# One comparison per candidate, batch-wise gate columns, and another order of the last batch's steps, between attention and its experts

## The chip, the core and the metric

The kernel runs on one core of a Trainium2 chip. The core has five engines with instruction queues of their own: TensorE (PE: matrix multiplications; its loads of weights are shown apart, as PEld), VectorE (DVE), ScalarE (ACT), GpSimd (POOL) and SyncE (SP, which here only issues transfers). Each engine works through its queue in order. SBUF is the working memory of 128 partitions, PSUM holds what TensorE writes, and HBM holds inputs, outputs and the scratch `xs`. The metric is the device time of one execution in microseconds.

## The reference

Block-causal attention over 8 batches of 8 heads, 576 positions and 64 columns, and behind it a mixture of 8 experts, in which each token goes to one expert and each expert keeps at most 80 tokens, those with the largest gates. `x` is attention's output, as 4608 tokens of 512 columns.

```
scores = scale * np.matmul(q, k.transpose(0, 1, 3, 2))
mask = block_i >= block_j                      # blocks of 64 positions
scores = np.where(mask, scores, -1000000000.0)
attn = np.exp(scores - max);  attn = attn / (sum(attn) + 1e-09)
x = np.matmul(attn, v)                         # (4608, 512) after a transpose
...
logits = x @ w_gate
expert_idx = np.argmax(logits, axis=1)
gate_w = softmax(logits)[np.arange(N), expert_idx]
for e in range(E):
    tok_idx = np.where(expert_idx == e)[0]
    if len(tok_idx) > capacity:
        keep = np.argpartition(-gw, capacity)[:capacity]
        tok_idx = tok_idx[keep]
    h = np.maximum(x[tok_idx] @ w1[e], 0.0)
    out[tok_idx] = gate_w[tok_idx, None] * (h @ w2[e])
```

All other rows of the output are zero.

## The kernel before

**Attention.** Two heads form a pair; 32 pairs go through a software pipeline. A table of steps (`TURN`, `LAST` for the last pair) sets the order in which the code issues each step of the pairs in flight: transposes of q and k on VectorE, scores on TensorE, row maxima on VectorE, exponentials on ScalarE, transposes of the probabilities on TensorE, their copies out of PSUM on ScalarE or VectorE (`take`, line 784), products with v. At "t" in the table (function `t`, line 843) a batch's small steps of the gate run one at a time, from the list `small`. A pair's result is transposed on VectorE (`flip`, line 407) and four transfers per batch, on SyncE's queue, store it in `xs` (`store_x`, line 420). The softmax's division is not done there: `xs` also gets the reciprocals of the sums.

**Gates.** For each batch the logits per token are made (`products`, `shift`, `expo`), the chosen expert is marked (`first_of`: `eq` is 1 for the first largest) and the gate weighted (`weight`). `turn` or, for the last batch, `turn_gated` spreads gates over lanes into the tile `sp`, and `turn2` brings them by matmuls to PSUM, so that 16 partitions hold one expert's gates. `placed` (line 578) copies them into `Wt`. `Wt` has the gates of all batches in two halves h of 160 columns, in the order t, batch, a.

**Router, from line 971.** After the last batch, per partition and half: MAX8 takes the 8 largest gates of 160 (line 981), 6 of them are candidates, 12 in all (`NCAND`). Their places come from max_index (line 1011). `spread` and six matmuls (line 1004) put all 192 candidates of an expert next to each other in PSUM. For each candidate one pass counts the larger ones, six on VectorE (line 1049) and six on ScalarE (line 1053, a sum of signs, which is twice the count and an offset). The count, with a penalty for empty candidates and an order among equals (`pen`), is the slot. `one_hot` compares three candidates' slots at a time with 0 to 79 (line 1060, fp32, result bf16). Twelve matmuls with these (line 1079) pick per slot and expert the token's number, split in RI's parts hi and lo, which GpSimd makes from the place by shifts, products and sums. Line 1083 adds them: `gi`.

**Gathers and the start of the experts.** GpSimd gathers an expert's 80 rows of `xs` by `gi` (`fetch`, line 1093), for experts 0, 1 and 2 at once. VectorE splits the gates in three bf16 parts, TensorE picks them with the same one-hots (line 1120), ScalarE copies the result (gsum) and VectorE sums it to `comb` (lines 1133 and 1134). `divide` (line 1197) multiplies an expert's gathered rows by the reciprocals: four instructions each. For expert 0 these are ordered behind the sum in `comb` (line 1263), and four transposes, four copies on ScalarE and 64 matmuls follow, piece by piece. For expert 1 (`split`, line 1256) nothing in the code holds them behind expert 0's; the framework's scheduler places them, and all other instructions of this part, in VectorE's queue. `finish_` (line 1145) makes flags (`ids`, `vm`, `chk`, `dif`) that tell whether the 12 candidates were enough; if not, a general path runs. It doesn't run here.

**Experts.** For each: 128 matmuls with w1, ScalarE's relu, the matmuls with w2, a gated sum and a scatter on GpSimd's queue. Weights come in 2 MB transfers on SyncE's queue, three of the sixteen during attention, the first of the others behind the gather of expert 0.

**Warm-ups.** `warm` (line 788) issues matmuls of no use, 512 columns each, between steps of the router. `WARM` lists how many: at the kernel's start, behind the turn of batch 6, of batch 7, behind the ranking, behind the pick of tokens and behind the pick of gates; `WARM_PICK` stands in the middle of the pick.

## Time and profile before

| | |
|---|---|
| median of 3 runs | 382.70 us (382.64 to 382.75) |
| the profiled execution | 382.09 us, span 380.4 us |
| attention | to about 273.5 us |
| router, to expert 0's first matmul | 273.5 to 290.9 us |
| experts | 290.9 to 374 us |
| last scatter, to the end | from 375.05 us |
| busy share of the span | TensorE 96%, VectorE 75%, ScalarE 75%, GpSimd 48% |

The span is the time from the first to the last recorded instruction; the execution has 1.7 us around it. Times in the views are microseconds from the span's start. A line of the timeline gives the start, the busy time, engine, line, operation, output and inputs, how many instructions are merged, and in brackets how long the engine sat idle before it and what released it. Merged instructions overlap, so that two can be busy for less than the sum of both. In the windows PEclk is the clock that TensorE was granted, as a share of 2.4 GHz.

### The profile page before, as it was taken

What the parts mean: (1) busy time and instruction counts of PE and PEld (TensorE: products, weight loads), DVE (VectorE), ACT (ScalarE), POOL (GpSimd) and SP (SyncE); (2) the same over time, 40 slices, a digit from 0 to 9 for tenths busy, and PEclk for the clock granted to TensorE, in tenths of its full rate; (3) what the DMA queues carried; (4) which work ended last, traced back from release to release, by engine and by line L of the source; (5) the groups of instructions that cost most, each with busy time, mean ns of one, the idle gap of its engine ahead of it and who ended that gap; (6) DMA issues with size and microseconds to landing.
All of it is one profiled execution on the core that took longest, in us unless ns stands there. A gap on an engine that the chain in (4) does not pass through costs nothing.

```text
span 380.4 us, 15167 instructions
## 1 busy us (share of the span) xinstructions
PE 366.7 (96%) x5973; PEld 247.5 (65%) x5973; DVE 285.9 (75%) x804; ACT 286.9 (75%) x880; POOL 181.0 (48%) x373
## 2 busy tenths in 40 slices
PE   5899999999999999999999999999999999999993
PEld 3666667676676776676676676667667555666661
DVE  5889999999999999999999999999985311111001
ACT  1799999999999999999999999999521332322331
POOL 6346665656976766786577664431133112220000
PEclk9999999999999999999999999999999999999998
DMA  9979999999999999999999999999965999999940
GB/s 125 155 122 157 141 163 152 204 188 124 190 228 146 200 197 198 165 146 247 167 171 215 184 155 137 244 396 416 264 127 175 385 391 393 401 397 393 407 188 26
DMA packets 166272, 84.42 MB, mean 222 GB/s; under 512 B 132509, under 2 KB 151805, under 8 KB 166192
## 3 DMA queue, kind: packets, MB, share of 16 engines
q1 hardware_dynamic: 154768, 61.80, 75.4%
q0 software_dynamic: 9056, 21.27, 23.9%
q8 instruction: 49, 0.80, 1.0%
q10 hardware_dynamic: 2368, 0.30, 0.6%
q14 instruction: 31, 0.25, 0.3%
HBM read 63.21 MB, written 20.33 MB: 220 GB/s over the span
## 4 chain that ended last, share of the span: by engine, by line
PE 85%; DVE 8%; ACT 3%; DMA 2%; issue 1%; POOL 0%; POOLq 0%; ACTq 0%; SPq 0%; DVEq 0%
PE bank L764 21%; PE bank L657 20%; PE bank L738 13%; PE av L1321 9%; PE ps L1236 9%; PE bank L432 2%; PE bank L769 2%; DMA ld<-in_q_dram 2%; ACT P L704 2%; DVE raw L693 2%; DVE negm L693 1%; PE ps L796 1%; PE bank L674 1%; PE pm L1321 1%; DVE T L633 1%; PE bank L446 1%
## 5 line engine op out<-in xcount | busy, mean ns | idle before, releaser
L704 ACT ACTIVATE P<-bank,negm 128x512 f32<-128x512 f32 (+3 forms) x320 | 157.2, 546 | 9.1 <-DVE negm L693 5.8
L657 PE MATMUL bank<-T,qt 64*128 64x320 f32 (+3 forms) x512 | 98.8, 494 | 0.1
L764 PE MATMUL bank<-PT,vn 128*64 128x64 f32 (+3 forms) x1288 | 88.9, 292 | 0.0
L693 DVE TENSOR_REDUCE negm<-bank 128x1 f32<-128x320 f32 (+2 forms) x192 | 83.3, 472 | 6.2 <-PE bank L683 6.1
L786 ACT COPY PT<-bank 128x512 f32<-128x512 f32 x149 | 77.0, 633 | 3.3 <-PE bank L738 2.8
L764 PEld LDWEIGHTS bank<-PT,vn 128*64 128x64 f32 x1288 | 57.1, 137 | 26.8 <-ACT PT L786 3.4
L640 POOL TENSOR_SCALAR qt<-T 128x128 f32<-128x128 f32 (+2 forms) x96 | 31.1, 342 | 89.3 <-DVE T L633 89.3
L738 PEld LDWEIGHTS bank<-ident,P 64*128 64x128 f32 (+1 forms) x1600 | 57.9, 137 | 11.7 <-issue 6.6
L738 PE MATMUL bank<-ident,P 64*128 64x64 f32 (+1 forms) x1600 | 63.4, 225 | 1.3 <-ACT P L704 0.6
L657 PEld LDWEIGHTS bank<-T,qt 64*128 64x128 f32 x512 | 47.9, 187 | 25.4 <-ACT PT L786 15.8
L704 ACT ACTIVATION_READ_ACCUMULATOR P<-bank,negm 128x1 f32 x256 | 61.0, 238 | 0.0
L693 DVE TENSOR_REDUCE raw<-bank 128x1 f32<-128x64 f32 (+1 forms) x128 | 51.7, 443 | 2.2 <-PE bank L657 1.9
L633 DVE STREAM_TRANSPOSE T<-ld 128x576 f32<-128x576 f32 x64 | 49.0, 765 | 2.8 <-DMA ld<-in_q_dram 1.6
L626 POOL DMA_DIRECT2D vn<-in_v_dram x58 | 45.8, 792 | 0.6 <-issue 0.4
L1321 PE MATMUL av<-w,hT 128*32 128x512 f32 (+3 forms) x320 | 39.3, 554 | 0.0
L618 POOL DMA_DIRECT2D ld<-in_k_dram x54 | 37.4, 699 | 2.7 <-DMA ld<-in_q_dram 2.7
L1330 DVE SCALAR_TENSOR_TENSOR y<-av,comb,yt 80x512 f32<-80x512 f32 (+1 forms) x8 | 5.6, 696 | 42.0 <-ACT yt L1328 41.9
L1236 PE MATMUL ps<-xsT,w 128*64 128x80 f32 x896 | 32.6, 233 | 0.0
L1236 PEld LDWEIGHTS ps<-xsT,w 128*64 128x64 f32 x896 | 31.4, 138 | 1.4 <-issue 0.9
L1336 POOL DMA_INDIRECT out_dram<-y,si x8 | 7.5, 942 | 51.9 <-DVE y L1330 38.8
L1328 ACT ACTIVATE yt<-ps,gfar 32x512 f32<-32x512 f32 (+2 forms) x18 | 11.4, 634 | 24.5 <-PE ps L1321 24.4
L786 DVE COPY PT<-bank 128x512 f32<-128x512 f32 x43 | 29.2, 682 | 0.3
(203 smaller groups left out, 421.2 us busy)
## 6 DMA issues: line engine op xcount, KB each, us to landing
w<-in_moe_w_dram SPq DMA_DIRECT2D x13, 2048.0 KB, 15.8
xs<-Y SPq DMA_DIRECT2D x32, 288.0 KB, 6.4
out_dram<-zero SPq DMA_DIRECT2D x18, 512.0 KB, 8.2
ld<-in_q_dram SPq DMA_DIRECT2D x126, 72.0 KB, 5.3
vn<-in_v_dram POOLq DMA_DIRECT2D x58, 128.0 KB, 4.9
w<-in_moe_w_dram POOLq DMA_DIRECT2D x12, 512.0 KB, 7.2
ld<-in_k_dram SPq DMA_DIRECT2D x72, 72.0 KB, 5.1
ld<-in_k_dram POOLq DMA_DIRECT2D x54, 72.0 KB, 6.2
```

What stands on the lines that cost most here:

```text
L618: eng.dma_start(self.nat[x][r], (q, k)[x][b, h0 + h, :, 32 * i:32 * i + 32] .rearrange("(g r) d -> r g d", r=32))
L626: eng.dma_start(self.vn[:, h], v[b, h0 + h, 0:512].rearrange("(j p) d -> p j d", p=P))
L633: nc.vector.transpose(t, self.nat[x].rearrange("p g d -> p (g d)"))
L640: nc.gpsimd.tensor_scalar(qb[:, to], tb[:, of], scalar1=SCALE, scalar2=1.0, op0=ALU.mult, op1=ALU.mult)
L657: nc.tensor.matmul(s[h][:, c:c + n], lhsT=q_[:, P * t - BLK:P * t + BLK], rhs=k_[:, 0:n], start=(c == 0 and g != "2"), stop=(g == "1"))
L693: nc.vector.tensor_reduce(to[:, b, h:h + 1], self.s[g][h][:, c:c + n], axis=AX.X, op=ALU.max, negate=True)
L704: nc.scalar.activation(Pt[self.i % 2][u][:, h, c1:c1 + n], self.s[g][h][:, c:c + n], AF.Exp, bias=self.negm[:, t, h:h + 1], scale=1.0, acc ...
L738: nc.tensor.transpose(pt[c][0:cols.stop - cols.start, n_ * BLK:(n_ + 1) * BLK], row[u][r, h, cols], ident[r, r])
L764: nc.tensor.matmul(a4[r] if c0 is None else av[r, BLK * c0:BLK * (c0 + b1 - b0)], lhsT=self.vn[:, h, j, :], rhs=self.PT[:, h, row, b0:b1]. ...
L786: (nc.scalar.copy if (eng or TAKE[x]) == "a" else nc.vector.tensor_copy)(*self.out.pop(x))
L1236: last = nc.tensor.matmul(dst(b)[64 * c:64 * (c + 1)], lhsT=w_[:, a, cols], rhs=x_[a], start=(a == 0), stop=(a == n - 1))
L1321: last = nc.tensor.matmul(to[col:col + s1 - s0, c0:c1], lhsT=hT[:, a, s0:s1], rhs=w_[:, a, c0:c1], start=(a == ends[0]), stop=(a == ends[1 ...
```

## The change

- **Columns.** `Wt` now has 18 columns per half and batch, a batch's side by side: 144 per half, and 8 more behind them. After the batch before the second last is placed, MAX8 over the first six batches' 108 columns goes into these 8 (`best_early`, in the list of small steps). After the last batch MAX8 reads the last two batches' 36 columns and those 8. With this order the place times 32 plus a constant of the partition and half is the token's number, so the shifts and two of RI's parts go; the constants (`iota_b`, `order_c`, two parts of `RI`) are made on GpSimd in `constants3`, at pair 7.
- **Comparisons.** One instruction for each candidate subtracts the count from 0 to 79 (or from the even numbers, for ScalarE's sums) in bf16 and compares with the penalty. `slot` is made later, for two candidates, in `finish_`.
- **Last values.** ScalarE copies the first 256 columns and the last 64, VectorE the second 256. x's last transpose stands ahead of the products, and x is stored in two parts of four transfers each. The gate sum (`weighed`) stands ahead of the index (`found`), and the last `sp` is a tile of its own.
- **Warm-ups.** Three numbers of `WARM` are smaller, and `WARM_PICK` goes.

```
-WARM = [8, 8, 5, 9, 8, 9]
+WARM = [8, 8, 3, 7, 8, 5]
-WARM_PICK = 2
...
+        half = NCAND // 2
+        for h in range(2):
+            nc.gpsimd.tensor_scalar(iota_b[:, h], iota_s, scalar1=1.0 + h, scalar2=0.0, op0=ALU.mult, op1=ALU.add)
+            nc.gpsimd.tensor_scalar(order_c[:, h], iota_c[:, 0:half], scalar1=1.0 + h, scalar2=16.0 * NCAND * h,
+                                    op0=ALU.mult, op1=ALU.add)
+        sb = sameE.unsqueeze(1).broadcast_to([P, NCAND, E])
+        nc.gpsimd.tensor_copy(RI[:, :, 2], sb)
+        nc.vector.tensor_scalar(iota_r16, iota_r, scalar1=16.0, scalar2=None, op0=ALU.add)
...
-        def store_x(self):
+        def store_x(self, g0=0, g1=S // 32):
...
-            self.sp = sp = sm.tile([P, E, NT, 8], F32, name="sp", bufs=1)
+            self.sp = sp = sm.tile([P, E, NT, 8], F32, name="sp_last", bufs=1)
...
+    NB = S // 32
+    HW = NB * B
+    early_b = max(B - 2, 1)
+    Wt = sel.tile([P, 2, HW + 8], F32, name="Wt")
+    Wf = Wt[:, :, 0:HW]
+
+    def best_early():
+        for h in range(2):
+            yield nc.vector.max(Wt[:, h, HW:HW + 8], Wt[:, h, 0:NB * early_b])
...
+            if bt.b == early_b - 1:
+                fill(best_early)
...
         bt.flip(NP - 1, 0, 8)
-        pairs[n - 1].take("V01", "a")
-        pairs[n - 1].take("V1", "v")
+        bt.store_x(0, 8)
+        pairs[n - 1].take("V01", "v")
+        pairs[n - 1].take("V1", "a")
+        bt.flip(NP - 1, 8, S // 32)
+        bt.store_x(8)
...
-        bt.flip(NP - 1, 8, S // 32)
-        bt.store_x()
...
-        for g_ in (found, found, found, weighed, found, weighed):
+        for g_ in (found, found, weighed, found, weighed, found):
             next(g_)
...
-        vec.max(cand16[:, h], Wf[:, h * HW:(h + 1) * HW])
+        vec.max(cand16[:, h], Wt[:, h, NB * early_b:])
...
-    hot = vec.tensor_tensor(slot[:, 0:NV], cnt_v, pen_[:, 0:NV], op=ALU.add)
-    for c0 in (0, 3):
+    hot = counted
+    for i in range(NCAND):
+        h, c = divmod(i, NH)
         with tc.issue_after(hot.ins):
-            hot = one_hot(c0, c0 + 3)
...
+            hot = vec.tensor_scalar(OH[:, i], iota_b[:, h], scalar1=(cnt_v, cnt_a)[h][:, c:c + 1],
+                                    scalar2=pen[:, h, c:c + 1], op0=ALU.subtract, op1=ALU.is_equal)
...
+        slot = sel.tile([P, 2], F32, name="slot")
+        for h in range(2):
+            vec.tensor_scalar(slot[:, h:h + 1], (cnt_v, cnt_a)[h][:, NH - 1:NH], scalar1=pen[:, h, NH - 1:NH],
+                              scalar2=(1.0, 0.5)[h], op0=ALU.add, op1=ALU.mult)
```

The scheduler also gives the queues another order. The first place is VectorE's queue after the gates' split, in the kernel before. The numbers tell tiles apart: xg_6165 holds the gathered rows of expert 0, xg_6166 those of expert 1; xn0 and xn are their quotients.

```order
L1133 TENSOR_TENSOR comb_6221<-gsum_6225 80x8
L1134 TENSOR_TENSOR comb_6221<-comb_6221,gsum_6225 80x8
L1203 TENSOR_TENSOR xn0_0_6251<-xg_6165 80x128
L1203 TENSOR_TENSOR xn0_1_6252<-xg_6165 80x128
L1203 TENSOR_TENSOR xn0_2_6253<-xg_6165 80x128
L1203 TENSOR_TENSOR xn0_3_6254<-xg_6165 80x128
L1203 TENSOR_TENSOR xn_6307<-xg_6166 80x128 x4
L1141 COPY gfar_6222<-comb_6221 32x8 x2
```

The same place in the changed kernel, where xg_6168 is expert 0's and xg_6169 expert 1's:

```order
L1199 TENSOR_TENSOR xn_6306<-xg_6169 80x128 x4
L1140 CAST ids_6319<-gi_6160 80x8
L1146 TENSOR_SCALAR vm_6325,nval_6324<-cand_6059 128x12
L1150 TENSOR_SCALAR slot_6328<-cnt_v_6089,pen_6082 128x1
L1150 TENSOR_SCALAR slot_6328<-cnt_a_6090,pen_6082 128x1
L1160 MEMSET dif_6336 128x8
L1125 TENSOR_TENSOR comb_6220<-gsum_6224 80x8
L1179 TENSOR_SCALAR comb_6220<-ids_6319 80x8
L1147 TENSOR_SCALAR chk_6323<-sameE_114,nval_6324 128x8
L1152 TENSOR_TENSOR chk_6323<-slot_6328,cap_133 128x2
L1126 TENSOR_TENSOR comb_6220<-comb_6220,gsum_6224 80x8
L1199 TENSOR_TENSOR xn0_0_6250<-xg_6168 80x128
```

Expert 1's four divides have moved from behind expert 0's to the front, and ten small instructions of `finish_` and of the sum stand between.

The second place is VectorE's queue from the counts to the index, before:

```order
L1049 TENSOR_SCALAR junk,cnt_v<-av,cand 128x192 x6
L1063 TENSOR_TENSOR slot<-cnt_v,pen 128x6
L1060 TENSOR_TENSOR OH<-slot,iota_s 128x240 x2
L1068 SCALAR_TENSOR_TENSOR slot<-cnt_a,pen 128x6
L1060 TENSOR_TENSOR OH<-slot,iota_s 128x240 x2
L1083 TENSOR_REDUCE gi<-ps 80x8
```

And after it:

```order
L1030 MAX_INDEX cidx<-cand,Wt 128x8 x2
L1053 TENSOR_SCALAR junk,cnt_v<-av,cand 128x192 x6
L1065 TENSOR_SCALAR OH<-iota_b,cnt_v,pen 128x80 x6
L1065 TENSOR_SCALAR OH<-iota_b,cnt_a,pen 128x80 x6
L1075 TENSOR_REDUCE gi<-ps 80x8
```

Six instructions have become twelve, without a slot in between, and the three shifts that stood ahead of the counts are gone.

## Rows read from the trace of the kernel before

**Rows 1.** The page's first part: busy us of each engine, share, instructions.
```profile
PE 366.7 (96%) x5973; PEld 247.5 (65%) x5973; DVE 285.9 (75%) x804; ACT 286.9 (75%) x880; POOL 181.0 (48%) x373
```

**Rows 2.** Windows by stage: us, then each engine's busy us, PEclk, DMA share, GB/s.
```profile
240.00:265.00 25.00, 24.88 (x420) 16.95 (x418) 23.39 (x65) 23.89 (x76) 7.94 (x16) 1.00 1.01 356
283.00:284.00 1.00, 0.94 (x7) 0.47 (x5) 0.86 (x5) 1.00 (x7) 0.00 (x0) 1.00 0.62 119
284.00:285.00 1.00, 0.97 (x8) 0.50 (x8) 0.64 (x3) 0.39 (x2) 0.00 (x0) 1.00 0.00 0
340.00:350.00 10.00, 10.00 (x180) 6.11 (x176) 1.56 (x5) 3.34 (x6) 0.94 (x1) 1.00 1.03 394
377.00:378.00 1.00, 0.00 (x0) 0.00 (x0) 0.00 (x0) 0.00 (x0) 0.00 (x0) 0.64 0.28 76
```

**Rows 3.** Chain that ended last, from 290.5 us: start, us, what.
```profile
373.96 0.37 DVE yt L1326
```

**Rows 4.** Waits of TensorE from 291 to 373 us: total, times, longest.
```profile
PE ps L1223 <- ACT x L1272: 0.2, 1, 0.2
```

**Rows 5.** Timeline of VectorE, attention's end: start, us, line, operation, idle before.
```profile
267.93 0.68 DVE L786 COPY PT<-bank 128x512 f32<-128x512 f32 x1
...
273.79 0.23 DVE L786 COPY xT<-bank 128x64 f32<-128x64 f32 x1
274.23 0.60 DVE L467 TENSOR_TENSOR prod__112<-bank,rs 128x80 f32<-128x80 f32 x3 [0.21 <-PE bank L446]
274.69 0.50 DVE L409 STREAM_TRANSPOSE Y<-xT 128x320 f32<-128x320 f32 x1
```

**Rows 6.** Timeline of VectorE, last batch's gates to the first MAX8.
```profile
276.74 0.20 DVE L492 TENSOR_REDUCE ix<-eq 128x5 f32<-128x40 f32 x1
276.85 0.19 DVE L499 TENSOR_REDUCE g<-dl 128x5 f32<-128x45 f32 x1
...
277.64 0.56 DVE L562 TENSOR_TENSOR sp<-eq,gs 128x160 f32<-128x160 f32 x2
...
278.86 0.55 DVE L981 MAX8 cand<-Wt 128x8 f32<-128x160 f32 x2
```

**Rows 7.** Timeline of all engines, last counts to the index of tokens.
```profile
283.05 0.08 DVE L1049 DVE_READ_ACCUMULATOR junk<-av,cand 128x1 f32 x1
...
284.16 0.23 ACT L1053 ACTIVATION_READ_ACCUMULATOR junk<-ps,keyn 128x1 f32 x1
...
284.69 0.73 DVE L1060 TENSOR_TENSOR OH<-slot,iota_s 128x240 bf16<-128x240 f32 x2
...
285.79 0.17 DVE L1083 TENSOR_REDUCE gi<-ps 80x8 int32<-80x16 f32 x1 [0.38 <-PE ps L1079]
```

**Rows 8.** Groups by line, 283 to 293 us: count, busy, mean ns, idle.
```profile
L1060 DVE TENSOR_TENSOR OH<-slot,iota_s 128x240 bf16<-128x240 f32 x4 | 1.5, 404 | 0.1
```

**Rows 9.** Timeline of all engines, first gather to expert 0's first matmuls.
```profile
286.25 1.13 POOL L1094 DMA_INDIRECT xg<-xs,gi  x1 [3.45 <-DVE gp L1108]
...
288.23 2.33 PE L796 MATMUL ps<-identr 128*128 128x512 f32 x9
...
289.50 0.90 DVE L1203 TENSOR_TENSOR xn<-xg 80x128 f32<-80x128 f32 x4 [0.52 <-DMA xg<-xs,gi]
...
290.39 0.37 PE L1271 MATMUL pm<-ident,xn 80*128 80x80 f32 x3
...
290.99 0.89 DVE L1203 TENSOR_TENSOR xn<-xg 80x128 f32<-80x128 f32 x4 [0.59 <-DMA xg<-xs,gi]
...
292.50 0.17 DVE L1148 CAST ids<-gi 80x8 f32<-80x8 int32 x1
...
292.82 0.22 DVE L1155 TENSOR_SCALAR chk<-sameE,nval 128x8 bf16<-128x8 f32 x1
```

**Rows 10.** Timeline of TensorE at the kernel's start.
```profile
4.19 3.78 PE L796 MATMUL bank<-identr 128*128 128x512 f32 x8 [4.19 <-DVE identr L229]
```

**Rows 11.** Timeline of SyncE's queue: the last batch's x, stored.
```profile
275.21 5.08 SPq L423 DMA_DIRECT2D xs<-Y  x4
```

More of the change, by code (lines that the diff above doesn't have):

```diff
@@ L277, in tile_attn_moe @@
     iota_s = const.tile([P, CHUNK], F32, name="iota_s")
+    iota_r16 = const.tile([P, 1], F32, name="iota_r16")
+    iota_b = const.tile([P, 2, CHUNK], BF16, name="iota_b")
+    order_c = const.tile([P, 2, NCAND // 2], F32, name="order_c")
+    RI = const.tile([P, NCAND, 3, E], BF16, name="RI")
     iota_p = const.tile([P, 1], F32, name="iota_p")
@@ L329, in constants3 @@
         nc.vector.tensor_reduce(iota_r, iota_c16, axis=AX.X, op=ALU.add)
+        half = NCAND // 2
[6 more added lines that the diff above has]
+        nc.vector.tensor_scalar(iota_r16, iota_r, scalar1=16.0, scalar2=None, op0=ALU.add)
+        for h, r_ in enumerate((iota_r, iota_r16)):
+            nc.gpsimd.tensor_scalar(RI[:, half * h:half * (h + 1), 1], sb[:, half * h:half * (h + 1)], scalar1=r_, scalar2=1.0,
+                                    op0=ALU.mult, op1=ALU.mult)
         nc.vector.scalar_tensor_tensor(cap, cf[:, 1:2], 4294967296.0, cf[:, 0:1], op0=ALU.mult, op1=ALU.add)
@@ L786, in take, with warm @@
             (nc.scalar.copy if (eng or TAKE[x]) == "a" else nc.vector.tensor_copy)(*self.out.pop(x))
-    def warm(n, wt, after=None):
+    def warm(n, wt, after=None, wide=4):
         if not n:
@@ L795, in warm @@
             for i in range(n):
-                last = nc.tensor.matmul(wt.rearrange("p (a c) -> p a c", c=P), lhsT=identr,
-                                        rhs=identr.unsqueeze(1).broadcast_to([P, 4, P]), start=(i == 0),
+                last = nc.tensor.matmul(wt[:, 0:wide * P].rearrange("p (a c) -> p a c", c=P), lhsT=identr,
+                                        rhs=identr.unsqueeze(1).broadcast_to([P, wide, P]), start=(i == 0),
                                         stop=(i == n - 1))
@@ L980, in tile_attn_moe @@
     for h in range(2):
-        vec.max(cand16[:, h], Wf[:, h * HW:(h + 1) * HW])
+        vec.max(cand16[:, h], Wt[:, h, NB * early_b:])
     pall = [ps_a.tile([P, 512], F32, name="av"), ps_s.tile([P, 512], F32, name="ps")]
     spreads = []
-    near = sel.tile([P, 2, NCAND], F32, name="near")
     spread = sel2.tile([P, 2, 2, 16, NH], F32, name="spread")
@@ L1010, in tile_attn_moe @@
         for h in range(2):
-            vec.max_index(cidx[:, h], cand16[:, h], Wf[:, h * HW:(h + 1) * HW])
+            vec.max_index(cidx[:, h], cand16[:, h], Wf[:, h])
     HOLD = 0
@@ L1037, in per_expert @@
         return eng.tensor_tensor(dst, part.unsqueeze(2).broadcast_to([P, NCAND, E]), sb, op=ALU.mult)
-    per_expert(RI[:, :, 0], hi_)
-    per_expert(RI[:, :, 1], lo_)
-    pool.tensor_copy(RI[:, :, 2], sb)
-    slot = sel.tile([P, NCAND], F32, name="slot")
+    per_expert(RI[:, :, 0], at)
     NV = NH
@@ L1075, in tile_attn_moe @@
     for i in range(NCAND):
-        with ExitStack() as order:
-            if i == NV:
-                order.enter_context(tc.issue_after(warm(WARM_PICK, wt[:, 1], picked).ins))
-            picked = nc.tensor.matmul(pick[0:CHUNK, 0:3 * E], lhsT=OH[:, i], rhs=RI[:, i].rearrange("p k e -> p (k e)"),
-                                      start=(i == 0), stop=(i == NCAND - 1))
+        picked = nc.tensor.matmul(pick[0:CHUNK, 0:3 * E], lhsT=OH[:, i], rhs=RI[:, i].rearrange("p k e -> p (k e)"),
+                                  start=(i == 0), stop=(i == NCAND - 1))
     gi = sel2.tile([CHUNK, E], I32, name="gi")
@@ L1392, in tile_attn_moe @@
         mid = gen.tile([P, 1], F32, name="mid")
-        many = gen.tile([P, NW], BF16, name="many")
+        many = gen.tile([P, 2, HW], BF16, name="many")
         cnt = gen.tile([P, 1], F32, name="cnt")
```

45 lines of the change are left out of this document (9 added, 36 removed).

## The prediction, made before the result was known

> **What bounds the kernel now.** I read the page first, then the windows by stage, then the chain of waits, then the timeline of the stretch that the change touches. The page shows TensorE busy for 96% of the span, and VectorE and ScalarE for 75% [rows 1]. The windows tell the stages apart: in late attention TensorE is busy 24.88 of 25 us and VectorE 23.39, and from 340 to 350, among the experts, TensorE is busy all the time, with the other engines mostly free [rows 2]. The chain ends with VectorE's last instructions on the last matmuls' result, at 373.96 [rows 3], and the scatter; and from 291 to 373 us TensorE, which runs the experts without a break, waits 0.2 us in all [rows 4]. So whatever moves the start of expert 0's matmuls moves the end by the same amount. Between attention's end (273.5) and that start lies the router's stage, a serial chain through VectorE, TensorE, ScalarE and GpSimd. Nearly the whole change lies there.
>
> **The change part by part.** I count microseconds of the profiled execution; minus is earlier.
>
> Inside attention. The batch-wise columns keep the instruction per batch and its size (36 columns for 40). New are two MAX8 over 108 columns, at most 0.55 by the pair over 160 [rows 6], one small VectorE instruction and seven on GpSimd. GpSimd's run in mid-attention, where its queue has idle time. VectorE has 1.6 us idle in 25, and TensorE sets the pace there [rows 2], so the MAX8 can cost 0 to 0.5. They also push the last index steps two slots back, so one 0.2 us reduction comes later, just before attention's end. I take +0.1.
>
> Last values, flip, products. VectorE's copy grows from 64 to 256 columns. 64 take 0.23 and 512 take 0.68 [rows 5], so 256 take about 0.42, which is +0.19. The flip of 0.50 now runs before the products, so it fills the 0.21 in which VectorE waited between the copy's end at 274.02 and its products. Copy from 273.79, flip to about 274.75, three products 0.15 apart, and the fourth at about 275.2 instead of some 0.05 before the flip's end at 275.19 [rows 5]: +0.1, between -0.1 and +0.25. Gate sum before index: g stood behind the index reduction, at 276.85 instead of 276.74 or a little before [rows 6]. From g to the spread (sp) are three dependent steps, through the reciprocal and gs: a 0.20 instruction and some 0.03 to the next. With g at 276.70, the reciprocal ahead of the index comparison, and the spread in a tile of its own (no waits for TensorE and GpSimd on the old one), sp starts at 276.70 + 3 x 0.23 = 277.39 instead of 277.64 [rows 6]: -0.25, between 0 and -0.3.
>
> Last MAX8: 44 columns instead of 160. The four one-hots mean 0.404, and two take 0.73 together [rows 7, 8], so the next 240 columns start 0.33 later. Eight-column instructions start about 0.07 apart [rows 9]. That makes about 0.07 and 1.05 ns per column. The two MAX8 fall from 0.55 by 116 columns each, -0.24; the first ranking matmuls wait for this.
>
> One comparison per candidate. VectorE is through its counts at 283.05, ScalarE at 284.39; then came a slot (0.17) and two one-hots (0.73), to 285.42, and the index at 285.79 [rows 7]. Now twelve comparisons of 80 columns follow VectorE's counts. At 0.07 + 80 x 1.05 ns they start 0.155 apart: the last starts at 283.05 + 11 x 0.155 = 284.75 and ends at 285.0. That is -0.42, and -0.07 because one matmul is left behind the last comparison, not three. Bounds: -0.85 if the comparisons keep up with ScalarE (the last starts at 284.44), -0.1 if a scalar column slows each by 0.03. The three index shifts go too, but VectorE then waited for the ranking matmuls anyway: 0. GpSimd's shorter chain to RI ends earlier than before: 0.
>
> The rows show the old 240-column one-hots, two fp32 inputs, at 1.05 ns per column [rows 8]. The Trainium skill ("VectorE: DVE Perf Modes", section "What auto-detection actually checks") says that an instruction with one 16-bit source and a 16-bit destination in SBUF can take a mode with four times the columns per cycle; the new comparison has that form. No row here shows it. By it the comparisons would start 0.09 apart and ScalarE would bound them: -0.85 instead of -0.49.
>
> Sum up to the gather of expert 0, by the rows: +0.1 + 0.1 - 0.25 - 0.24 - 0.49 = **-0.8** (between 0 and -1.3). The first gather issues at 285.45, and the data that let VectorE start at 289.50 and 290.99 [rows 9] are there at 288.7 and 290.19.
>
> What is behind it costs more. Before, VectorE's queue reads gate sum, expert 0's four divides, expert 1's four. Now expert 1's four come first, at the head of the queue, with a wait for the second gather. Behind that wait stand ten small instructions and then expert 0's divides, though their gather landed 1.49 earlier. Working: expert 1's divides start at 290.19, the fourth 0.61 later (four take 0.89 [rows 9]); the small ones begin 0.2 after it, at 291.0. From 292.50 to 292.82 there are seven starts, 0.05 apart [rows 9]; with an accumulator read and some waits I take 11 x 0.07 = 0.77. Expert 0's first divide starts at 291.77 instead of 289.50. Not all of those 2.27 count. Before, the divide was done at 289.79, but TensorE still worked through nine warm-up matmuls and took up the transposes at 290.39 [rows 9]. Now only five follow the gate pick, 0.26 each from 288.23 - 0.8, and are over at about 288.8. The transposes start at 291.77 + 0.29 + 0.06 = 292.12, which is **+1.73**. From there expert 0 runs as before, and nothing later can take it back: TensorE has no slack [rows 2, 4], and weights, which start after gather 0, come 0.8 earlier. Bounds: 0.5 for small instructions and -1.3 for the sum give +0.95; 1.2 and 0 give +3.0.
>
> The profiled execution took 382.09 (span 380.4, and 1.7 around it), 0.61 under the median of 382.70. 382.09 + 1.73 = 383.8 on its scale, **384.4** as a median.
>
> Nothing is gained or lost by the store of x in two parts: its traffic ends between 283 and 284 [rows 2], and the gather waits for the index until after 285. Fewer warm-ups elsewhere only keep TensorE free for what it waits for.
>
> **The rivals.**
> - *TensorE's clock falls.* TensorE is idle from about 288.8 to 292.1, longer than anywhere between the first matmul and the last. The one place of before like it is the end: VectorE takes the last matmuls' result at 373.96 [rows 3], and the granted clock is 0.64 over 377 to 378 [rows 2], so it falls from 2.4 to 1.2 GHz within that microsecond. At the kernel's start eight warm-ups took 3.78 us, 0.47 each [rows 10], against 0.26 for nine at 288.23 [rows 9]. If expert 0 begins with 3.8 us at that pace, it loses 3.8 - 3.8 x 0.26 / 0.47 = 1.7: 386.1. Against it: the granted clock is 1.00 in every stretch read from attention to the experts [rows 2], and the five warm-ups still fill the first part of the wait.
>  The Trainium skill ("TensorE: Matmul & The Clock Gate", section "HAM oscillation — how this bites in real kernels") says that a wait for DMA between groups of matmuls can throttle TensorE again, so that the next group starts slow. The trace before has no such wait, so it can't say.
> - *The order costs nothing*: the second gather comes with the first, or the wait before expert 1's divides isn't for it. Then expert 0's divide starts at 288.7, the transposes at 289.05, free of warm-ups: -1.34, 381.4. Against it: the second gather's divides started 1.49 after the first's, though VectorE was free from 290.4 on [rows 9].
> - *Within the noise*: comparisons at the fast pace, small instructions at 0.05, the whole router 1.3 shorter: +0.5 to +0.95, 383.2 to 383.6.
> - *The store in eight transfers holds the gather.* SyncE's four took 5.08 to issue, to 280.29 [rows 11], and their traffic ended some 3.5 later [rows 2]. At a fixed price per transfer eight take 10.2 from about 275.0, to 285.2; the traffic would end at 288.7 and hold a gather due at 285.45 by 3.2: 387.6. It decides once that traffic lasts past 285.4. Against it: the bytes and the pieces are the same, and the first four no longer wait for the second flip.
>
> **How the numbers follow.** The forecast has 0.57, the clock 0.20, no cost 0.10, noise 0.09, the store 0.04. A measurement can't tell less than 0.2%, 0.77 us, from no change. Slower: 0.57 + 0.20 + 0.04, 0.81; faster: 0.10; same: 0.09. The range leaves out the faster case, the store and the outer part of the clock's: 383.2 to 386.4.
>
> **What would show it.** Right: VectorE's L1199 for expert 1 starts before expert 0's, with idle time released by the gather, and the ten small ones between; TensorE idle some 3 us before L1267; the index near 285.0; expert runs as before. Comparisons 0.09 apart speak for the fast mode. Wrong: expert 0's transposes start before 290.4 on the trace, or matmuls of expert 0 run at half pace (the clock), or the gathers wait for x's stores.

## The result and the profile after

The changed kernel takes 387.04 us (median) against 382.73 for the kernel before, run beside it: a ratio of 1.0102, 95% interval 1.0075 to 1.0129. It is slower, as forecast, and its median lies 0.6 above the predicted range. By the ratio the loss is 3.9 us, where 1.7 were forecast. One of its six runs, 392.93, was in the chip's slow state, and the ratio uses the other five, whose median of 386.38 lies at the upper end of the range. The profiled execution took 386.38, its span 384.7 instead of 380.4 us.

Where the 4.3 us of the two profiled executions lie, read as differences of the same steps' starts (the last count at its end), stage by stage:

| stretch | before | after | difference |
|---|---|---|---|
| start to attention's end (a copy of the last pair, [rows 5]) | 267.93 | 270.59 | +2.66 |
| from there to the sum of the last batch's products | 7.48 | 7.60 | +0.12 |
| to the first MAX8 [rows 6] | 3.45 | 3.20 | -0.25 |
| to VectorE's last count [rows 7] | 4.27 | 4.09 | -0.18 |
| to the index [rows 7] | 2.66 | 2.88 | +0.22 |
| index to expert 0's first transposes [rows 9] | 4.60 | 7.08 | +2.48 |
| from there to the end | 90.0 | 89.3 | -0.7 |

For the last line the other kernels' profiles show 89.4 to 90.1 where the clock stays at 1.00 from there on, with no edit in that stage, so most of the -0.7 is such spread.

The page's first part, answering to [rows 1], shows the same shares:

```profile
PE 367.5 (96%) x5963; PEld 247.6 (64%) x5963; DVE 286.1 (74%) x812; ACT 287.2 (75%) x880; POOL 181.3 (47%) x373
```

The timeline of VectorE and one row of SyncE, answering to [rows 5], [rows 6], [rows 7] and [rows 11] (start, busy us, engine, line, operation, output and inputs, count, idle before):

```profile
276.49 0.42 DVE L803 COPY xT<-bank 128x256 f32<-128x256 f32 x1
277.02 0.51 DVE L423 STREAM_TRANSPOSE Y<-xT 128x320 f32<-128x320 f32 x1
277.45 0.70 DVE L481 TENSOR_TENSOR prod__112<-bank,rs 128x80 f32<-128x80 f32 x4
277.55 5.20 SPq L437 DMA_DIRECT2D xs<-Y  x8
...
279.45 0.20 DVE L513 TENSOR_REDUCE g<-dl 128x5 f32<-128x45 f32 x1
279.56 0.18 DVE L506 TENSOR_REDUCE ix<-eq 128x5 f32<-128x40 f32 x1
...
280.14 0.59 DVE L576 TENSOR_TENSOR sp_last<-eq,gs 128x160 f32<-128x160 f32 x2
...
281.39 0.31 DVE L1001 MAX8 cand<-Wt 128x8 f32<-128x44 f32 x2
...
285.40 0.08 DVE L1053 DVE_READ_ACCUMULATOR junk<-av,cand 128x1 f32 x1
285.40 1.36 DVE L1065 TENSOR_SCALAR OH<-iota_b,cnt_v,pen 128x80 bf16<-128x80 bf16 x6
...
286.67 1.35 DVE L1065 TENSOR_SCALAR OH<-iota_b,cnt_a,pen 128x80 bf16<-128x80 bf16 x6
...
288.36 0.17 DVE L1075 TENSOR_REDUCE gi<-ps 80x8 int32<-80x16 f32 x1 [0.34 <-PE ps L1071]
```

The copy of 256 columns took the 0.42 that was forecast, and the flip stands ahead of all four products. The gate sum g stands ahead of ix, and MAX8 takes 0.31 for the pair. Six comparisons start at 285.40 and the next six at 286.67: 0.21 apart, not 0.155. The eight stores of x took 5.20 to issue, as the four did.

Then the order that was forecast, TensorE and GpSimd among it, answering to [rows 9]:

```profile
288.17 3.57 PE L813 MATMUL ps<-identr 128*128 128x512 f32 x8
...
288.82 1.12 POOL L1086 DMA_INDIRECT xg<-xs,gi  x1 [5.09 <-DVE gp L1100]
...
293.44 0.89 DVE L1199 TENSOR_TENSOR xn<-xg 80x128 f32<-80x128 f32 x4 [3.24 <-DMA xg<-xs,gi]
294.26 0.16 DVE L1140 CAST ids<-gi 80x8 f32<-80x8 int32 x1
...
295.02 0.16 DVE L1126 TENSOR_TENSOR comb<-comb,gsum 80x8 f32<-80x8 f32 x1
295.10 0.89 DVE L1199 TENSOR_TENSOR xn<-xg 80x128 f32<-80x128 f32 x4
...
295.44 0.69 PE L1267 MATMUL pm<-ident,xn 80*128 80x80 f32 x3 [2.01 <-DVE xn L1199]
```

Expert 1's divides wait 3.24 for the second gather; the small instructions follow, 294.26 to 295.10; expert 0's divides come last, and TensorE sits idle for 2.01. Eight warm-ups at 288.17 took 3.57, where they take 2.09 at the full clock. The windows (us; PE, PEld, DVE, ACT, POOL busy, PEclk, DMA share, GB/s) show why:

```profile
286.00:287.00 1.00, 0.98 (x5) 0.54 (x5) 1.00 (x6) 0.74 (x4) 0.00 (x0) 1.00 0.00 0
287.00:288.00 1.00, 0.98 (x6) 0.56 (x5) 1.00 (x5) 0.00 (x0) 0.00 (x0) 0.98 0.00 0
288.00:289.00 1.00, 1.00 (x4) 0.83 (x4) 0.63 (x5) 0.16 (x1) 0.18 (x1) 0.50 0.00 0
...
291.00:292.00 1.00, 1.00 (x15) 0.78 (x14) 0.00 (x0) 0.00 (x0) 0.69 (x2) 0.82 0.32 125
...
340.00:350.00 10.00, 10.00 (x178) 5.94 (x176) 1.14 (x6) 3.34 (x6) 1.92 (x2) 1.00 1.03 395
```

TensorE's granted clock fell to half (1.2 of 2.4 GHz) at 288, after the twelve token picks, and was back at 1.00 from about 291.4. In this execution that is hidden: VectorE waits for the second gather until 293.44 anyway. The experts run as before, without a wait [rows 2, 4].

Inside attention two stretches stand out. TensorE has one gap that no wait explains and that the kernel before doesn't have (its waits, 135 to 143 us: total, times, longest):

```profile
PE bank L755 <- issue: 1.3, 1, 1.3
```

And in front of batch 6's products on VectorE stands now a reciprocal that before was done earlier. Before:

```profile
255.14 0.38 DVE L405 RECIPROCAL rs<-rs 128x40 f32<-128x40 f32 x1
...
258.44 0.76 DVE L409 STREAM_TRANSPOSE Y<-xT 128x576 f32<-128x576 f32 x1
259.35 0.68 DVE L467 TENSOR_TENSOR prod<-bank,rs 128x80 f32<-128x80 f32 x4
```

And after, where TensorE waits for the products:

```profile
261.15 0.17 DVE L418 TENSOR_SCALAR rs<-sums 64x8 f32<-64x8 f32 x1
261.35 0.40 DVE L419 RECIPROCAL rs<-rs 128x40 f32<-128x40 f32 x1
261.86 0.68 DVE L481 TENSOR_TENSOR prod<-bank,rs 128x80 f32<-128x80 f32 x4
...
262.39 0.82 PE L755 MATMUL bank<-ident,P 64*128 64x64 f32 x11 [0.30 <-DVE prod L481]
```

### The profile page after: what moved, and what is told of

Same layout as the page of the kernel before. It is cut to its first block, busy times and chain, and to the rows that moved or that the text cites. A ratio compares the mean times of both kernels' runs of the same rounds, so it can differ in the third digit from the quotient of the medians.

```text
span 384.7 us, 15155 instructions
## 1 busy us (share of the span) xinstructions
PE 367.5 (96%) x5963; PEld 247.6 (64%) x5963; DVE 286.1 (74%) x812; ACT 287.2 (75%) x880; POOL 181.3 (47%) x373
## 4 chain that ended last, share of the span: by engine, by line
PE 71%; DVE 12%; DMA 7%; issue 3%; SPq 2%; ACT 2%; POOL 1%; POOLq 0%; ACTq 0%; DVEq 0%
PE bank L781 17%; PE bank L674 16%; PE bank L755 10%; PE av L1317 10%; PE ps L1232 9%; DVE negm L710 3%; DMA ld<-in_q_dram 3%; DVE raw L710 3%; PE bank L446 2%; ACT P L721 2%; DVE T L650 2%; SPq L635 2%; PE bank L786 2%; DMA vn<-in_v_dram 1%; DMA vt<-in_v_dram 1%
## 5 line engine op out<-in xcount | busy, mean ns | idle before, releaser
L657 POOL TENSOR_SCALAR qt<-T 128x128 f32<-128x128 f32 (+2 forms) x96 | 31.1, 343 | 89.4 <-DVE T L650 89.3
```

The costliest lines, as they stand in the source:

```text
L657: nc.gpsimd.tensor_scalar(qb[:, to], tb[:, of], scalar1=SCALE, scalar2=1.0, op0=ALU.mult, op1=ALU.mult)
```

## The experiments

All times are medians; each ratio is to the kernel before, run beside it on the same chip, with its 95% interval. Not all were run on the same chip, so the ratios are what can be compared. The last column is the time in us from the start of the index to that of expert 0's first transposes, in the one profile of each.

| kernel | us | ratio | index to transposes |
|---|---|---|---|
| changed, again | 387.61 | 1.0102 [1.0050, 1.0154] | 7.40 |
| 1 expert 0's divides first | 383.01 | 1.0005 [0.9980, 1.0030] | 4.02 |
| 2 warm-ups of before | 383.92 | 1.0031 [1.0007, 1.0055] | 4.46 |
| 3 both | 383.79 | 1.0020 [1.0004, 1.0035] | 4.62 |
| 4 kernel before, expert 1 first | 385.31 | 1.0067 [1.0036, 1.0097] | 6.23 |
| 5 warm-ups of before, expert 1 first | 385.61 | 1.0062 [1.0030, 1.0095] | 6.18 |
| 6 as 1, early MAX8 late | 381.91 | 0.9967 [0.9937, 0.9997] | 5.02 |
| 7 as 1, three at a time | 382.43 | 0.9977 [0.9945, 1.0010] | 3.98 |
| 8 mixed comparisons | 380.63 | 0.9939 [0.9915, 0.9963] | 3.88 |
| 9 three at a time | 381.32 | 0.9955 [0.9934, 0.9976] | 3.95 |
| 10 forms | 382.80 | 0.9994 [0.9966, 1.0023] | 3.80 |
| 11 long warm-up | 386.70 | 1.0103 [1.0066, 1.0140] | 7.05 |
| 12 constants late | 383.51 | 1.0007 [0.9984, 1.0030] | 3.86 |
| 13 order, clock kept | 385.97 | 1.0076 [1.0049, 1.0102] | 7.06 |
| 14 one scalar | 381.37 | 0.9957 [0.9927, 0.9987] | 3.99 |

**The changed kernel again** (no edit, beside 5 to 7).

> The changed kernel once more, unchanged, beside the others of this set. If the 4 us between it and the kernel with expert 0's divides first are the kernel's and not the chip's, the median is 386 to 388 and 1.0 to 1.3% above before. If the chip made them, about 385. In its profile the order puts expert 0's first transposes some 7.0 us behind the index, whether or not the granted clock falls at the token pick; attention ends 1.1 to 1.3 us later than before the change when the start-up is subtracted, unless a gap like the one of 1.29 at 138.7 shows again (2.5).

1.0102 again, so the loss is the kernel's and not a chip's. Attention ended 1.38 later than before the change; this splits into -0.6 by 43 us, +0.3 near 110, +0.9 at the gap near 138.7 and +0.76 between 256 and 268. In this profile the clock fell twice, the second time where the prediction's rival put it:

```profile
287.00:288.00 1.00, 1.00 (x4) 0.77 (x5) 0.87 (x6) 0.16 (x1) 0.52 (x1) 0.63 0.00 0
...
293.00:294.00 1.00, 0.00 (x0) 0.00 (x0) 1.00 (x12) 0.00 (x0) 0.00 (x0) 1.00 0.96 320
294.00:295.00 1.00, 0.58 (x3) 0.54 (x3) 0.97 (x8) 0.15 (x1) 0.00 (x0) 0.54 1.00 381
295.00:300.00 5.00, 5.00 (x68) 4.54 (x69) 0.49 (x3) 0.71 (x4) 0.00 (x0) 0.50 0.99 378
```

TensorE idle in 293 to 294, then expert 0 at half pace. ScalarE's first copy of expert 0 lies 4.19 later than before the change, its activation at 300.52 already 6.58: 2.4 lost. Each run has a mean granted clock. Of the eleven runs behind the two ratios of this kernel, the seven at 0.989 to 0.994 took 386.6 us on average and the four at 0.982 or 0.983, as in this profile, 388.5.

**1, expert 0's divides first.**

```
         with tc.issue_after(gated.ins):
-            divide(xn, xg[0])
+            divided_[0] = divide(xn, xg[0])
...
+        if e == 1:
+            order.enter_context(tc.issue_after(divided_[0].ins))
         divided_[e] = divide(xn_[e], xg[e])
```

> The changed kernel with one thing undone: expert 1's four divides are held behind expert 0's on VectorE, which gives its queue the order gate sum, expert 0's divides, expert 1's, small instructions, as before the change. Order theory: in the changed kernel's profile expert 0's divides start 3.03 us later behind the index than before the change; of that some 2.2 to 2.8 us come back, so the time falls from 387.0 to about 384.5. Clock theory (the order is a detail, what costs is the granted clock, which fell to 0.50 at 287.96 for 3.4 us): the warm-ups and the gate pick still end late, the gate sum then sets the start of expert 0's divides, and at most 0.5 us come back: 386.5 or more. Under 383 would mean that attention's 2 us in the profile are no part of the loss.

```profile
291.59 0.89 DVE L1199 TENSOR_TENSOR xn<-xg 80x128 f32<-80x128 f32 x4 [0.48 <-DMA xg<-xs,gi]
...
291.93 0.69 PE L1270 MATMUL pm<-ident,xn 80*128 80x80 f32 x3 [0.18 <-DVE xn L1199]
```

The index came at 287.91, so the transposes start 4.02 behind it instead of 7.08. 3.7 of the 3.9 us are gone (1.0102 to 1.0005), more than the order theory's 2.8; the clock theory's 386.5 is refuted. The two profiles show 3.06 of them between index and transposes. What the rest is, this run doesn't show; without the idle stretch ahead of expert 0 there is also none in which the clock could fall.

**2 and 3, the warm-ups of before, without and with that order.**

```
-WARM = [8, 8, 3, 7, 8, 5]
+WARM = [8, 8, 5, 9, 8, 9]
+WARM_PICK = 2
```

> The changed kernel with the warm-ups of before: 8, 8, 5, 9, 8, 9 and two in the middle of the token pick. The order on VectorE stays as changed. Clock theory: the granted clock stays at 1.00 up to the experts, mean clock 0.996 instead of 0.982 to 0.994, the runs agree within 0.5 us instead of 2.4, and the median falls by 1 to 2 us, to 385 to 386. Order theory: VectorE waits for the second gather anyway, which hides the warm-ups' slow pace; the median stays at 386.5 to 387.

> The changed kernel with both: expert 0's divides first and the warm-ups of before. If order and clock are all of the loss behind the router, expert 0's divides start some 3.7 us behind the index as before the change (289.50 against 285.79), and the time is 382.7 plus what attention and router lost: 2.6 us by the profile, 385.3, if these are real; 382.9 if attention's 2 us belong to that one execution; below 382.5 if the comparisons gain as forecast.

Kernel 2 took 383.92, against both theories: with these warm-ups the scheduler itself puts expert 0's divides first, so 2 and 3 have the same order. Of the numbers that differ, two more warm-ups behind the ranking, or the two in the token pick, turn VectorE's queue round in the built program; those behind batch 7 or the gate pick don't (11 has more there and keeps the changed order). Experiment 2 thus doesn't separate clock and order; 4, 5 and 13 bear on that. In 3 the divides start 3.72 behind the index, as expected, and the time, 383.79, lies between its cases.

**4, the order alone, in the kernel before.**

```
+        split(1)
-        with tc.issue_after(gated.ins):
+        with tc.issue_after(divided_[1].ins):
             divide(xn, xg[0])
```

> The kernel before with one thing changed: expert 1's four divides ahead of expert 0's four on VectorE, both behind the gate sum; the small instructions stay behind both. Order theory: the divides of expert 1 start with the second gather's data at 290.99, expert 0's at about 291.62 instead of 289.50, the transposes at about 291.97 instead of 290.39, and nothing takes it back: +1.6 us, 384.3. The other side (a late start is absorbed, or the gathers' spacing shrinks): within 0.3 us of 382.7.

```profile
290.62 1.70 DVE L1203 TENSOR_TENSOR xn<-xg 80x128 f32<-80x128 f32 x8 [1.89 <-DMA xg<-xs,gi]
...
291.77 0.69 PE L1272 MATMUL pm<-ident,xn 80*128 80x80 f32 x3 [1.46 <-DVE xn L1203]
```

The transposes start 6.23 behind the index, +1.63 as expected, with the clock at 1.00 throughout, and the time rises by 0.67%, 1.4 to 3.7 us. Eight divides in one row: expert 0's wait behind expert 1's. So the late start by the order alone is shown. How much of the 0.67% is the order's is not: TensorE idles 1.46 here too, and the three runs with a mean granted clock of 0.997 or more took 383.1 to 383.6, four others, at 0.987 to 0.994, 385.1 to 387.2 (the kernel before beside them 383.0). So a part of this cost goes with the clock, and three runs are too few to tell the rest. 13 against 3, below, gives the order's price with the clock kept.

**5, the same order in the changed kernel with the warm-ups of before** (edits of 2 and 4).

> The changed kernel with the warm-ups of before, and expert 1's divides forced ahead of expert 0's (the ten small instructions stay behind both). Against the same without the force (383.9, where the scheduler puts expert 0's first): order theory +1.6 to 1.9, 385.6, with the transposes 6.2 us behind the index instead of 4.46. If the order costs only in company with fewer warm-ups (by the clock): 384.0.

1.0062 against 1.0031 without the force, 385.61 as expected; 6.18 behind the index. The intervals overlap, and the mean granted clock of these runs lies between 0.987 and 0.999, so a part may again be the clock's.

**6, the early MAX8 out of the list of small steps** (with 1).

```
-            if bt.b == early_b - 1:
-                fill(best_early)
...
         while small:
             t()
+        for _ in best_early():
+            pass
         for _ in bt.placed():
```

> The changed kernel with expert 0's divides first, and the two MAX8 over the first six batches taken out of the list of small steps and put behind the last spread, where VectorE waits 0.27 for TensorE. Theory: in the list they pushed batch 6's reciprocal of the sums (0.17 and 0.40) right in front of its products, on which TensorE waits, and that cost 0.6 to 0.7 between 258 and 265. Then this comes back (the shift against before stays the same from 255 to 268 instead of growing by 0.73), the two MAX8 cost at most 0.1 at the new place, and the time is some 0.6 below the kernel with them in the list: 382.4 if that is 383.0. Rival: the growth between 258 and 265 comes from GpSimd or from transfers and stays; 383.0.

```profile
258.21 0.76 DVE L423 STREAM_TRANSPOSE Y<-xT 128x576 f32<-128x576 f32 x1
259.11 0.68 DVE L481 TENSOR_TENSOR prod<-bank,rs 128x80 f32<-128x80 f32 x4
```

No reciprocal stands ahead of the products. The shift against before stays at -0.24 from 256 to 273 us, where it grows by about 0.76 in all nine profiles with the two MAX8 in the list. At the new place the two MAX8 cost nothing: sum of products to last MAX8 takes 3.20 as before the move. In this profile the clock fell in the token pick, at 285.2, and here it wasn't hidden: the gate sum was copied 3.95 behind the index, not 2.63, and expert 0's divides started 0.8 later behind it than in 1. The time, 381.91, is 1.5 us below that of 1 by the ratios, where 0.6 were expected; the intervals overlap.

**7, three candidates at a time** (with 1).

```
-            hot = vec.tensor_scalar(OH[:, i], iota_b[:, h], scalar1=(cnt_v, cnt_a)[h][:, c:c + 1],
-                                    scalar2=pen[:, h, c:c + 1], op0=ALU.subtract, op1=ALU.is_equal)
+    hot = vec.tensor_tensor(slot3[:, 0:NV], cnt_v, pen[:, 0], op=ALU.add)
+    for c0 in (0, 3):
+        hot = one_hot(c0, c0 + 3)
+    hot = vec.scalar_tensor_tensor(slot3[:, NV:], cnt_a, 0.5, penh, op0=ALU.mult, op1=ALU.add)
+    for c0 in (NH, NH + 3):
+        hot = one_hot(c0, c0 + 3)
```

> The changed kernel with expert 0's divides first, and the comparisons as before the change: slots first, then four instructions of three candidates each, fp32 against fp32. If twelve single comparisons 0.22 apart gain nothing over four of 0.404, the index comes 2.7 us behind VectorE's last count as before the change, instead of 2.9 to 3.0, and the time is the same within 0.3 us: 382.8. If the singles gain the 0.49 that was forecast, this is 0.5 slower: 383.5.

The index is 2.66 behind VectorE's last count, with the singles 2.84 (2.82 to 2.88 in nine profiles). The singles are 0.2 slower, not 0.49 faster. The time can't be told from that of 1, as expected.

**8, 9 and 10: mixed, three at a time, and forms**, all with the edits of 1 and 6 and two warm-ups in the pick. 8 has:

```
+    hot = vec.tensor_tensor(slot3[:, 0:NV], cnt_v, pen[:, 0], op=ALU.add)
+        hot = one_hot(0, NV)
+    for i in range(NV, NCAND):
...
```

with the singles of the changed kernel for ScalarE's six; 9 has the lines of 7; 10 has

```
+        for s0, s1 in ((0, CHUNK // 2), (CHUNK // 2, CHUNK)) if i < 3 else ((0, CHUNK),):
+                if 3 <= i < NH:
+                    hot = vec.tensor_scalar(OH[:, i], iota_b[:, 0], scalar1=slot3[:, i - 3:i - 2], scalar2=None,
+                                            op0=ALU.is_equal)
...
+                    hot = vec.tensor_scalar(OH[:, i, s0:s1], (iota_2 if NH <= i < NH + 3 else iota_b[:, h])[:, s0:s1], scalar1=one,
```

> Expert 0's divides first, the early MAX8 behind the last spread, two warm-ups back in the middle of the token pick, and the comparisons mixed: VectorE's six counts in one instruction of 480 columns (fp32) behind a slot, ScalarE's six one by one. At 0.57 for the 480 columns, 0.17 for the slot and 0.22 for each single, the last comparison starts 1.84 to 1.9 behind VectorE's last count instead of 2.5, and the index comes at about 2.2 to 2.3 instead of 2.84. Time 0.5 below the kernel with singles only (381.9), and another 0.3 to 0.7 if the two warm-ups keep the granted clock at 1.00 and the gate sum ahead of the first gather: 380.8 to 381.4. If the start-to-start time is set by the instruction's end and not by its start, the index is only 0.2 earlier.

> As the one before, but the comparisons three at a time as before the change. Index 2.66 behind VectorE's last count, time 381.2 to 381.7. Against the kernel before it keeps the gate sum ahead of the index, the shorter MAX8, the flip ahead of the products, and neither late reciprocal nor changed divides: 0.26 + 0.21 + 0.1 earlier, and 0.3 to 0.4 from fewer warm-ups ahead of the transposes; the constants' 0.3 to 0.4 inside attention stay.

> Only a look at the price of forms, in the kernel with expert 0's divides first, early MAX8 late and two warm-ups in the pick. Candidates 0 to 2 are compared in two halves of 40 columns; 3 to 5 with one scalar column (a slot made first) instead of two; 6 to 8 with an fp32 source instead of bf16; 9 to 11 as in the changed kernel. Read from the trace as start-to-start times. If 0.22 is 0.07 + 0.155 by columns: halves 0.14 to 0.15 apart, fp32 the same as bf16. If it is a price per instruction (two scalar columns): halves 0.20 to 0.22 apart, one column 0.14 to 0.18. If a fast mode for 16-bit sources is at work and hidden by the scalars: fp32 sources clearly over 0.22, some 0.28.

VectorE in kernel 10:

```profile
283.10 1.29 DVE L1075 TENSOR_SCALAR OH<-iota_b,cnt_v,pen 128x40 bf16<-128x40 bf16 x6
284.30 0.53 DVE L1072 TENSOR_SCALAR OH<-iota_b,slot 128x80 bf16<-128x80 bf16 x3
284.75 0.77 DVE L1075 TENSOR_SCALAR OH<-iota,cnt_a,pen 128x80 bf16<-128x80 f32 x3
285.45 0.71 DVE L1075 TENSOR_SCALAR OH<-iota_b,cnt_a,pen 128x80 bf16<-128x80 bf16 x3
```

From one group's start to the next's: 40 columns, two scalars 1.20 / 6 = 0.20; 80 columns, one scalar 0.45 / 3 = 0.15; 80 columns fp32, two scalars 0.70 / 3 = 0.23; bf16, two scalars 0.21 (in the changed kernel 1.27 / 6). So 40 more columns cost 0.01, a second scalar column 0.06, and an fp32 source 0.02. The price is one per instruction. The columns are cheap: 0.01 for 40 is 0.25 ns each, which agrees with the mode of four times the columns per cycle in the Trainium skill ("VectorE: DVE Perf Modes", section "What auto-detection actually checks"), as far as 0.01 can tell. The sign expected of a fast mode, some 0.28 for an fp32 source, did not come. Either way the columns are the small part here.

The mixed kernel, VectorE:

```profile
282.83 0.17 DVE L1068 TENSOR_TENSOR slot<-cnt_v,pen 128x6 f32<-128x6 f32 x1
283.04 0.66 DVE L1065 TENSOR_TENSOR OH<-slot,iota_s 128x480 bf16<-128x480 f32 x1
283.61 1.35 DVE L1074 TENSOR_SCALAR OH<-iota_b,cnt_a,pen 128x80 bf16<-128x80 bf16 x6
285.26 0.17 DVE L1087 TENSOR_REDUCE gi<-ps 80x8 int32<-80x16 f32 x1 [0.30 <-PE ps L1083]
```

The index is 2.53 behind the last count, not the 2.2 to 2.3 expected: the slot starts 0.2 behind the start of the last count's read and the 480 columns another 0.2 later, where 0.17 was allowed for both, and the last of the twelve singles had started 2.3 behind it, not 2.5. 8 and 9 are faster than the kernel before, by 0.6% and 0.45%, close to what was expected of them; between them the intervals overlap.

**11, long warm-up**, in the changed kernel.

```
-WARM = [8, 8, 3, 7, 8, 5]
+WARM = [8, 8, 3, 7, 8, 14]
```

> The changed kernel with 14 instead of 5 warm-ups behind the gate pick, which fill TensorE's idle 2.0 to 2.25 ahead of expert 0's transposes; the order on VectorE stays as changed. Clock theory: part of the 387 is a clock that falls in that idle time (in the second profile of the changed kernel it was 0.50 from 294 to 300 and expert 0 lost 2.3); with TensorE busy it doesn't, and the median falls by 0.8 to 1.8, to 385.5 to 386.5, with a smaller spread. If the clock has no part in the median: 387.0 to 387.6 (up to 0.3 more where the warm-ups last past the divides).

1.0103: no gain. The warm-ups left 1.14 of idle time, and the clock fell all the same, at 295.2, 1.6 behind expert 0's first transposes; from the transposes to the end 91.2 us instead of 89.3 to 90. So this edit didn't keep the clock, and tells of its share only that expert 0 lost some 1.6 in this execution.

**12, constants late**, in 8: the new constants in a function of their own.

```
             if i == 7:
                 constants3()
+            if i == 22:
+                constants4()
```

> The kernel with mixed comparisons (380.6), and GpSimd's seven new constant instructions and their one on VectorE made at pair 22 instead of 7. If they cause the shifts that all kernels with the change show against before (0.1 at 74 to 79, 0.3 at 102 to 109, by a later weight and K transfer behind them on GpSimd's queue), these two go and something similar, 0.1 to 0.4, may come near pair 22 (some 195 to 210); where nothing comes, the time falls by 0.4, to 380.2. If the 0.3 at 109 stays, another part of the change makes it.

The 0.1 at 79 and the 0.3 at 109 are gone (shift -0.16 at 73 us, -0.12 at 117; in 8 from -0.59 to -0.17). So the constants made them. In the changed kernel VectorE waits there for a transfer of K, which it doesn't before; that this transfer is late by the constants ahead of it on GpSimd's queue is argued, not shown:

```profile
109.74 0.78 DVE L650 STREAM_TRANSPOSE T<-ld 128x576 f32<-128x576 f32 x1 [0.25 <-DMA ld<-in_k_dram]
```

At pair 22 they cost 1.5 instead: they stand ahead of a batch's spread on GpSimd, and TensorE waits for that (waits, 195 to 210 us):

```profile
PE bank L591 <- POOL sp L568: 1.5, 1, 1.5
```

The time, 383.51, missed the expected 380.2; by the ratios it is 0.68%, 2.6 us, above that of 8. These 1.5 are the part that the trace explains; its profile also has 1.0 at the gap near 138.7, where that of 8 has 0.2.

**13, the order with the clock kept** (warm-ups of 2, eight more behind the gate pick).

```
+        split(1)
+        small_ = divided_[1]
+        for i in range(10):
+            with tc.issue_after(small_.ins):
+                small_ = vec.tensor_scalar(spare[:, i:i + 1], iota_p, scalar1=1.0, scalar2=None, op0=ALU.mult)
-        with tc.issue_after(gated.ins):
+        with tc.issue_after(small_.ins):
             divide(xn, xg[0])
```

> The changed kernel, its order made by force (expert 1's divides, then ten small instructions that copy one column, then expert 0's divides), with the warm-ups of before and eight more behind the gate pick, so that TensorE is busy from the ranking to expert 0's transposes and the granted clock stays at 1.00. Transposes 6.9 to 7.1 us behind the index as in the changed kernel. Without a share of the clock: the same 1.0102 of before, 386.9 to 387.6. With it: lower by what the clock costs on the mean, 0.6 to 1.2 us, 1.007 to 1.0085 of before, 386.0 to 386.5, and fewer runs over 388.

TensorE's first transposes in 3 and in 13:

```profile
292.70 0.37 PE L1274 MATMUL pm<-ident,xn 80*128 80x80 f32 x3
```

```profile
293.35 0.69 PE L1277 MATMUL pm<-ident,xn 80*128 80x80 f32 x3 [0.47 <-DVE xn L1203]
```

They start 4.62 and 7.06 behind the index. In 13 the clock stayed at 1.00 until after the last matmul, and the time is 385.97, runs from 384.97 to 386.96 with a mean granted clock of 0.995 or more in each. Against 3, which has the same warm-ups up to the gate pick and the other order, 1.0076 stands to 1.0020: 0.56%, 2.1 us, and the intervals don't overlap. That is the order's price without the clock, near the 2.44 between index and transposes. Against 1.0102 twice, 13 is 0.26%, 1.0 us, lower: the clock's part. Here the intervals overlap (1.0049 to 1.0102, 1.0075 to 1.0129), so the size is an estimate; the 1.9 between the changed kernel's runs at either mean clock point the same way.

**14, one scalar**, in 8: GpSimd makes `mark_`, the numbers less the penalty.

```
-            hot = vec.tensor_scalar(OH[:, i], iota_b[:, 1], scalar1=cnt_a[:, c:c + 1],
-                                    scalar2=pen[:, 1, c:c + 1], op0=ALU.subtract, op1=ALU.is_equal)
+            hot = vec.tensor_scalar(OH[:, i], mark_[:, c], scalar1=cnt_a[:, c:c + 1], scalar2=None, op0=ALU.is_equal)
```

> The kernel with mixed comparisons, and ScalarE's six compared with one scalar column instead of two (GpSimd takes the penalty from the numbers 0, 2, ... beforehand, 480 columns, fp32). By the look at forms a single takes 0.152 instead of 0.211 from start to start with one column, and some 0.02 more with an fp32 source: 0.17. Index 2.53 - 6 x 0.04 = 2.25 to 2.3 behind VectorE's last count, time 380.3 to 380.4, which the measurement can hardly tell from 380.6. If VectorE has to wait for GpSimd's 480 columns, the index stays at 2.5 or comes later.

The index is 2.29 behind the last count, as expected; the time can't be told from that of 8.

## Why the prediction was wrong, step by step

The direction and the main mechanism, the order of the divides, were right; the size was not: 384.4 forecast, 387.04 measured. Two terms of the sum failed, the one inside attention and the one for the comparisons, and the clock, a rival, came on top in a part of the executions.

- **Order of the divides: right.** Forecast: expert 0's divides 291.77 - 285.0 = 6.77 behind the index, transposes 7.12. Measured 6.74 and 7.08. Experiments 1, 4 and 13 show that it costs by itself, and that nothing takes it back. What I missed is its cause: I wrote that fewer warm-ups "only keep TensorE free". They are what turned the scheduler's order round (2).
- **"Inside attention ... I take +0.1": failed**, the largest miss. I followed the two new small steps to the end of the list, saw one 0.2 reduction pushed back, and overlooked the reciprocal, 0.17 and 0.40, which they push in front of products that TensorE waits for: 0.76 (6). GpSimd's constants, said to run in idle time, cost 0.3 to 0.4, probably by the transfers behind them (12). Together 1.1, past the bound of 0.5. The rest of the profile's +2.66 can't be put down to these: 0.4 is there by 43 us, where other profiles, that of the kernel before in 4's order among them, lie between -0.6 and +1.1; and 1.1 comes at the gap near 138.7, whose cause stays open (below).
- **"One comparison per candidate ... -0.49": failed.** The term was taken as 0.07 + 80 x 1.05 ns from eight-column instructions and two-tensor one-hots. Columns are four times cheaper and the instruction three times dearer: 0.21 apart, so +0.2. My upper bound, a scalar column that adds 0.03, had the mechanism but half the size (10), and the comparison has two of them. Comparisons 0.09 apart, the sign of the fast mode, did not come either.
- Last values, flip and products +0.1: measured +0.12. Gate sum first -0.25: measured -0.25. Shorter MAX8 -0.24: measured -0.18 to -0.22 (from the first MAX8 to the last count).
- The sum's bounds, 0 to -1.3, were narrower than its terms' own bounds add up to (+0.4 to -1.5), and the lower bound of the comparisons, given as -0.85, is -0.80 by its own working. Measured by the change's own parts, the sum is about +1.0, outside both.
- **The clock: a rival, and part of the truth.** I gave it a chance of 0.20 and a price of 1.7. It fell in both profiles of the changed kernel, first in the token pick, which I hadn't considered, and in one of them also ahead of expert 0, at a price of 2.4. It doesn't replace the forecast but comes on top of it in some executions. The first fall is also why TensorE idled 2.01 and not some 3 ahead of the transposes: the warm-ups ran on until 293.4.
- The rival "the order costs nothing" is refuted by 1 and 4, "within the noise" by the result. The eight stores held nothing: they were issued in 5.20, and no traffic is left from 286 to 289 us, ahead of the gather at 288.82.

The sum with the measured terms: 384.4 + 1.0 (attention) + 0.7 (comparisons) = 386.1; the kernel with this order and the clock kept (13) measured 1.0076 of before, 385.6 on the scale of 382.7. The clock's part, about 1 by the same run, makes it 386.6 to 387.1. By its ratio of 1.0102 the changed kernel stands at 386.6 on that scale.

## What to carry to other kernels

Before costing a step as hidden, list what stands behind it in every queue it enters, to the next instruction that the bounding engine waits for; two MAX8 of 0.5 together cost 0.76 by what they pushed. Where a scheduler sets the order, a count of idle matmuls can reorder another engine: compare the built order, and pin the one dependence that matters. For these short comparisons the price was per instruction and per scalar column, so fewer and wider ones ended earlier even at a slower rate per column (8: the index 0.3 earlier).

## What the runs showed of the hardware, unexpected

- A VectorE comparison with scalar columns, in bf16, starts 0.15 behind the one before with one scalar column (80 columns) and 0.20 to 0.21 with two (40 and 80 columns).
- The granted clock fell at or behind the twelve token picks, during which TensorE has short matmuls and waits, in three of the six profiles without warm-ups in the pick (both of the changed kernel, and 6), and in none of the nine of its variants with two in it.
- TensorE shows a gap that no wait explains at one place of the program, near 138.7 us, of 0 to 1.3 us: 1.3 and 1.0 in the changed kernel, 0.2 in the kernel before with 4's order, none in the kernel before and in 1, 2, 6 and 9. No edit goes with it, and what makes it stays open.
